# Clearing the warm-up tile first, and spare matmuls in TensorE's waits for the quarters of batch 0's x

## The chip, the core and the metric

The kernel runs on one core of a Trainium2 chip. The metric is the device time of one execution in microseconds; the time of before is the median of seven runs. The engines are named as in the profile: PE is TensorE's matmuls and PEld its weight loads, DVE is VectorE, ACT is ScalarE, POOL is GpSimd, SP is SyncE, which here only issues DMAs.

## The reference

Two stages. The first is an attention between x and a small state, in both directions; the second is a feed-forward layer with a snake activation over all resulting tokens.

```python
B, H, S, Ns, D = (8, 8, 512, 32, 64)
# attention: x is (B, H, S, D), state is (B, H, Ns, D)
scores = x @ state.T / sqrt(D);  a = softmax(scores);   xread = a @ state
scores2 = state @ x.T / sqrt(D); a2 = softmax(scores2); sread = a2 @ x
attn_out = concatenate([xread, sread], axis=2)          # (B, H, 544, 64)
x = attn_out.transpose(0, 2, 1, 3).reshape(4352, 512)
# feed-forward: d_model 512, d_ff 2048
h = x @ w_in
s = np.sin(alpha * h)
g = h + s * s / (alpha + 1e-09)
return (g @ w_out).astype(np.float32)                   # (4352, 512)
```

## The kernel before

The work is cut into steps, each a method of `Steps` that issues a few instructions. The list `ORDER` names them in one sequence with their arguments (`xq.3.A` is `xq(3, "A")`); each engine and each queue executes its own instructions in the order of this list, and waits on semaphores for what other engines make. Capital letters choose an engine (A ScalarE, V VectorE, G GpSimd, S the SP queue), and the last number of a step that writes PSUM is one of eight banks. Each bank holds one tile at a time: the next tile in it waits until the one before is done with.

Tokens are processed in nine groups: one for each batch (512 tokens) and one of all state reads (256 tokens). For a batch, x is transposed, the scores against the state are made (`sc`), their exponential (`ex`), its row sums (`rs`), reciprocals (`rr`) and the normalised weights (`nm`). These are transposed (`at` and `ac` for batch 0). Instead of reading the state and then multiplying with w_in, the kernel multiplies the state with w_in (`m`, evicted by `me`), and `h` or `hg` multiplies the weights with that product, 128 columns of d_ff at a time. `si` is the sine, `sq` its square, `gt` the snake sum, `o` the product with w_out, `oc` and `os` the eviction and the store.

The head, which the change edits, gets batch 0 ready. Its steps:

- `touch_x`, `touch`, `l_alpha`: three small DMAs that ScalarE issues. `l_s01`: the state of batches 0 and 1, on SP. `lq.0` to `lq.3`: four quarters of batch 0's x (two heads each), on SP.
- `consts` (line 209): DVE clears the tile `warm`, the operand of the warm-up matmuls, and fills `ones`. `zero.0` and `zero.1` (line 214): DVE clears `stT`, the transposed state, in two parts. `ident_` makes the identity on POOL, `identf` casts a corner of it on DVE.
- `warm_up.n.cols.bank` (line 303): n matmuls of `cols` columns over the cleared tile, into a bank that nobody reads.
- `exp_table`, `sin_table`: ScalarE loads the table for the exponential, later that for the sine.
- `s01_c`, `s01_t`, `s01_k`: the state of batches 0 and 1 is cast (POOL), transposed (TensorE, line 309) and copied into `stT` by DVE and ScalarE (line 316).
- `xq.q.A` (line 356): ScalarE casts a quarter of x when it has landed; `xtq.q` (line 361): TensorE transposes it, four matmuls; `xc` (line 385): the result is copied out of PSUM by DVE or ScalarE.
- `al_t`, `al_c`, `inva`: alpha is transposed (line 320), copied and inverted (DVE). `st_t`, `st_c`: the rest of the state is transposed (line 333) and copied into `stT` (line 340).
- `l_st`, `li`, `lo`, `lx`: DMAs of the state, w_in, w_out and the next batch's x, issued on POOL.

In before the list begins with `zero.1` ahead of `consts`; the warm-up is three pairs of 128 columns and six of 512; between the quarters of x there are no spare matmuls, but after quarter 3 there are ten, and more follow later.

```python
def warm_up(k, n, cols, bank):
    wp = k.ps(bank, [k.P, k.S], FP32, "warm_ps")
    for _ in range(n):
        k.nc.tensor.matmul(wp[:, :cols], k.warm[:, 0:k.P], k.warm[:, :cols], start=True, stop=True)
```

Of the kernel before, what the change touches and what calls it, by code (L numbers as in the profile page):

```python
# [18 lines left out]


ORDER = """
touch_x l_s01 zero.1 touch lq.0.S ident_ consts warm_up.2.128.0 warm_up.2.128.1 warm_up.2.128.2
l_alpha lq.1.S zero.0 warm_up.6.512.3 exp_table lq.2.S identf.V lq.3.S s01_c.G l_st li.0 xq.0.A
s01_t.4 li.1 xtq.0.5 xq.1.A s01_k.1.V s01_k.0.A li.2 xtq.1.6 xc.0.0.0.V xq.2.A xc.0.0.1.V lo.0
al_t.7 xq.3.A xtq.2.0 al_c inva sc.0.0.1 lo.1 xc.0.1.0.A xtq.3.2 warm_up.2.128.3 ex.0.0
warm_up.2.128.4 lx.1.0.1 warm_up.2.128.5 xc.0.1.1.V warm_up.2.128.6 warm_up.2.128.7 rs.0.0 sc.0.1.0
li.3 st_t.0.3 ex.0.1 rr.0.0 st_t.1.4 lo.2 st_c.0.0.V st_c.0.1.A warm_up.2.128.5 warm_up.2.128.6
warm_up.2.128.1 st_c.1.0.A rs.0.1 warm_up.2.128.2 warm_up.2.128.7 nm.0.0.0.4.G warm_up.2.128.0
warm_up.2.128.5 st_c.1.1.A warm_up.2.128.3 warm_up.2.128.6 warm_up.2.128.1 rr.0.1 warm_up.2.128.2
sin_table warm_up.2.128.7 warm_up.2.128.0 nm.0.1.0.4.G at.0.0.5 warm_up.2.128.3 ac.0.0.V m.0.0.6.4  # L30
m.1.0.1.2 lo.3 at.0.1.7 me.0.0.0.V me.0.0.1.A warm_up.2.128.0 warm_up.2.128.3 me.1.0.1.A ac.0.1.V
hg.0.2.0.5 me.1.0.0.V hg.0.1.0.4 hg.0.2.1 hg.0.1.1 hg.0.0.0.0 lx.2.0.1 si.0.2 hg.0.0.1 m.1.1.6.3
si.0.1 m.0.1.7.2 hg.0.3.0.1 me.0.1.1.A sq.0.2.V hg.0.3.1 sq.0.1.G me.1.1.0.V me.1.1.1.A
warm_up.2.128.2 gt.0.2 si.0.0 warm_up.2.128.2 warm_up.2.128.6 warm_up.2.128.3 warm_up.2.128.2
warm_up.2.128.6 me.0.1.0.A gt.0.1 sq.0.0.G m.0.2.3.2 si.0.3 m.1.2.5.6 hg.0.4.0.7 me.0.2.0.V
me.0.2.1.A hg.0.4.1 sq.0.3.G hg.0.6.0.4 me.1.2.1.V hg.0.6.1 si.0.4 hg.0.7.0.3 hg.0.11.0.2 me.1.2.0.V
si.0.6 hg.0.7.1 sq.0.4.G hg.0.5.0.6 gt.0.0 hg.0.5.1 si.0.7 hg.0.11.1 hg.0.8.0.5 hg.0.8.1 sq.0.6.A
gt.0.3 sq.0.7.G o.0.3.0.2.0 si.0.5 gt.0.4 o.0.3.2.3 o.0.0.0.2.1 si.0.11 o.0.0.2.3 gt.0.6 sq.0.5.G
o.0.0.3.4 o.0.2.0.1.7 si.0.8 o.0.3.3.5 sq.0.11.A gt.0.7 hg.0.9.0.4 sq.0.8.G o.0.2.1.2 gt.0.5
o.0.2.2.4 hg.0.9.1 gt.0.11 o.0.0.4.5 hg.0.10.0.3 si.0.9 o.0.2.4.5 gt.0.8 o.0.0.5.6 o.0.3.5.6  # L40
sq.0.9.A o.0.3.6.8 pk.1.0.V hg.0.10.1 xt.1.1.6 pk.1.1.V si.0.10 gt.0.9 xt.1.0.2 xc.1.1.0.A sq.0.10.G
o.0.2.5.6 xc.1.1.1.V xc.1.0.0.A o.0.0.6.7 xc.1.0.1.V o.0.0.7.8 o.0.2.6.7 sc.1.1.5 gt.0.10 sc.1.0.4
m.0.3.6.2 ex.1.0 o.0.2.7.8 me.0.3.0.V o.0.1.0.3.3 me.0.3.1.V o.0.1.3.6 hg.0.13.0.6 o.0.1.6.7 ex.1.1
# [620 lines left out]
```

## Time and profile before

| | us |
|---|---|
| median of 7 runs | 221.27 |
| lowest, highest | 221.04, 222.78 |
| the seven runs | 221.04, 221.16, 221.16, 221.27, 221.8, 222.75, 222.78 |
| the profiled execution | 221.38 |
| its span, from the first to the last instruction | 219.5 |

The profile is of one execution. Times in it are counted from its first instruction; a row of the timeline gives the start, the length, the engine, the line, the operation with output and inputs, and in brackets the idle time before it and what ended that. A row of the chain of work gives the start, the length, and the engine and line that held the end back in that stretch. Rows of a stage give busy time with the number of instructions, the granted TensorE clock, the DMA share and GB/s. Matmuls are pipelined, so the length of one is more than the distance to the next.

The page's groups have the warm-up in one row, 66 matmuls in all:

```profile
L303 PE MATMUL warm_ps<-warm 128*128 128x128 bf16 (+1 forms) x66 | 7.4, 265 | 2.2 <-DVE warm L209 2.0
```

### The profile page before, as it was taken

The page shows a single profiled execution, that of the slowest core. Times are in us where ns is not written, and L with a number is a line of the kernel's source. Part 1 is how long each engine was busy: PE and PEld are TensorE (multiplying, and loading weights), DVE is VectorE, ACT ScalarE, POOL GpSimd, SP SyncE. Part 2 cuts the span into 40 slices and gives each one's busy share as a digit, 9 for nine tenths or more (in the row PEclk, how much of TensorE's full clock was granted, in tenths as well). Part 3 has the DMA queues.
Part 4 walks back from the last instruction along what each step waited for, and adds up shares of the span by engine and source line. Part 5 has one row for each costly group of instructions (what it writes and reads, how often), then busy time and mean ns, then how long its engine had stood idle before and what let it go on. Part 6 is the DMA issues. An engine that isn't in the chain of part 4 may idle for free.

```text
span 219.5 us, 4330 instructions
## 1 busy us (share of the span) xinstructions
PE 213.1 (97%) x1619; PEld 104.8 (48%) x1619; DVE 162.4 (74%) x286; ACT 173.6 (79%) x297; POOL 107.2 (49%) x115
## 2 busy tenths in 40 slices
PE   6899999999999999999999999999999999999994
PEld 2744544444444534444454444444444555665452
DVE  2769896999668889989888788888667987671201
ACT  3799878997899979898996999798858896685111
POOL 5958534795296647743943387273501082121000
PEclk9999999999999999999999999999999999999999
DMA  5999999935378529167135327470220211012042
GB/s 176 202 207 203 205 203 122 215 127 96 99 157 131 99 79 151 53 151 90 53 73 126 114 76 96 130 114 0 48 100 0 99 48 48 0 51 96 1 143 96
DMA packets 38052, 23.48 MB, mean 107 GB/s; under 512 B 20992, under 2 KB 33680, under 8 KB 38032
## 3 DMA queue, kind: packets, MB, share of 16 engines
q0 software_dynamic: 11648, 8.13, 26.3%
q1 hardware_dynamic: 26128, 15.08, 26.1%
q8 instruction: 12, 0.20, 0.4%
q14 instruction: 8, 0.07, 0.1%
q10 hardware_dynamic: 256, 0.01, 0.1%
HBM read 17.44 MB, written 8.91 MB: 120 GB/s over the span
## 4 chain that ended last, share of the span: by engine, by line
PE 95%; ACT 3%; DVE 1%; issue 0%
PE o_ps L587 54%; PE h_ps L537 22%; PE m_ps L488 4%; PE h_ps L543 3%; PE h_ps L552 3%; PE warm_ps L303 3%; PE s_ps L399 2%; PE w_ps L450 2%; PE w_ps L461 1%; ACT L226 1%; ACT s L560 1%; ACT M L496 1%; PE x_ps L376 0%; PE st_ps L333 0%; ACT stT L340 0%; PE x_ps L361 0%
## 5 line engine op out<-in xcount | busy, mean ns | idle before, releaser
L587 PE MATMUL o_ps<-w_out_sb,gT 128*128 128x512 bf16 (+2 forms) x560 | 137.7, 373 | 0.0
L576 DVE SCALAR_TENSOR_TENSOR gT<-s,inva_sb,h_ps 128x512 bf16<-128x512 bf16 (+1 forms) x144 | 96.6, 714 | 18.9 <-POOL s L201 9.5
L201 POOL TENSOR_TENSOR s<-s 128x512 bf16<-128x512 bf16 (+1 forms) x76 | 76.7, 1021 | 63.8 <-ACT s L560 62.0
L560 ACT ACTIVATE s<-h_ps,alpha_sb 128x512 bf16<-128x512 f32 (+1 forms) x144 | 88.8, 671 | 10.5 <-PE h_ps L543 4.3
L587 PEld LDWEIGHTS <-gT 128*128 128x128 bf16 x560 | 52.3, 98 | 60.3 <-issue 5.0
L537 PE MATMUL h_ps<-AT,M 128*128 128x512 bf16 x224 | 60.8, 379 | 0.0
L537 PEld LDWEIGHTS <-M 128*128 128x128 bf16 x224 | 21.7, 98 | 25.9 <-issue 0.4
L569 ACT ACTIVATE s<-s 128x512 bf16<-128x512 bf16 (+1 forms) x53 | 31.4, 595 | 0.8
L201 POOL TENSOR_TENSOR A<-E,rR 128x512 bf16<-128x512 bf16 x16 | 16.6, 1049 | 23.9 <-ACT o_sb L595 12.7
L595 ACT COPY o_sb<-o_ps 128x512 f32<-128x512 f32 (+2 forms) x24 | 13.7, 572 | 16.6 <-PE o_ps L587 16.5
L496 ACT CAST M<-m_ps 128x512 bf16<-128x512 f32 x35 | 18.6, 593 | 8.2 <-PE m_ps L488 8.1
L496 DVE CAST M<-m_ps 128x512 bf16<-128x512 f32 x29 | 18.9, 680 | 2.4 <-PE m_ps L488 2.1
L595 DVE COPY o_sb<-o_ps 128x512 f32<-128x512 f32 x11 | 7.6, 691 | 13.0 <-PE o_ps L587 12.9
L410 DVE TENSOR_REDUCE R<-E 128x16 f32<-128x512 bf16 x16 | 10.4, 658 | 1.2 <-ACT E L406 0.9
L201 DVE TENSOR_TENSOR s<-s 128x512 bf16<-128x512 bf16 (+1 forms) x15 | 6.2, 415 | 6.8 <-ACT s L560 6.7
L488 PE MATMUL m_ps<-w_in_sb,stT 64*32 64x512 bf16 x256 | 10.2, 382 | 0.0
L468 DVE RECIPROCAL rC<-w_ps 128x128 f32<-128x128 f32 x8 | 7.6, 948 | 3.3 <-PE w_ps L461 3.2
L552 PE MATMUL h_ps<-AT,M 128*128 128x512 bf16 x32 | 9.4, 380 | 0.4 <-ACT M L496 0.4
L303 PE MATMUL warm_ps<-warm 128*128 128x128 bf16 (+1 forms) x66 | 7.4, 265 | 2.2 <-DVE warm L209 2.0
L406 ACT ACTIVATE E<-s_ps 128x512 bf16<-128x512 f32 x16 | 8.8, 602 | 0.4 <-PE s_ps L399 0.3
L543 PE MATMUL h_ps<-xs_all,w_in_sb 128*128 128x256 bf16 x64 | 9.1, 273 | 0.0
L560 ACT ACT_TABLE_LOAD x5 | 6.4, 1283 | 2.2 <-PE h_ps L537 1.1
(56 smaller groups left out, 101.8 us busy)
## 6 DMA issues: line engine op xcount, KB each, us to landing
out_dram<-o_sb SPq DMA_DIRECT2D x33, 256.0 KB, 2.3
xnat<-in_x_dram POOLq DMA_DIRECT2D x7, 512.0 KB, 7.6
w_in_sb<-in_moe_w_in_dram POOLq DMA_DIRECT2D x4, 512.0 KB, 10.8
w_out_sb<-in_moe_w_out_dram POOLq DMA_DIRECT2D x4, 512.0 KB, 17.4
x<-in_x_dram SPq DMA_DIRECT2D x4, 256.0 KB, 4.6
st_nat<-in_state_dram POOLq DMA_DIRECT2D x1, 256.0 KB, 5.2
out_dram<-o_sb SPq DMA_DIRECT2D x1, 192.0 KB, 1.9
s<-in_state_dram SPq DMA_DIRECT2D x1, 128.0 KB, 2.3
```

Source lines behind the costliest of these rows:

```text
L201: {"V": k.nc.vector, "G": k.nc.gpsimd}[eng].tensor_tensor(out, a, b, ALU.mult)
L303: k.nc.tensor.matmul(wp[:, :cols], k.warm[:, 0:k.P], k.warm[:, :cols], start=True, stop=True)
L488: k.nc.tensor.matmul(k.t["m", b, s + n, g][o0:o0 + k.Ns, :], k.stT[k.half(r), b * k.G + g, c0:c0 + k.Ns], k.w_in_sb[k.half(r), 2 * g + h, ...
L496: k.copy(eng)(k.t["M", b][:, g, s * k.FW:(s + 1) * k.FW], k.t["m", b, s, g][:])
L537: k.nc.tensor.matmul(hp[:, :n], k.t["M", t][:, g, fs], k.t["AT", t][:, g, :], start=(g == 0), stop=(g == k.G - 1),)
L543: k.nc.tensor.matmul(hp[:, :n], k.w_in_sb[:, q, fs], k.xs_all[:, q].rearrange("p b j -> p (b j)"), start=(q == 0), stop=(q == k.Q - 1),)
L552: k.nc.tensor.matmul(k.t["h", t, f][:], k.t["M", t][:, g, f * k.P:(f + 1) * k.P], k.t["AT", t][:, g, :], start=(g == 0), stop=(g == k.G - 1),)
L560: k.nc.scalar.activation(s[:, :n], k.t["h", t, f][:, :n], ACT.Sin, scale=k.alpha_sb[:, f:f + 1])
L569: k.nc.scalar.activation(s2[:, :n], s[:, :n], ACT.Square)
L576: k.nc.vector.scalar_tensor_tensor(gT[:, :n], k.t["s2", t, f][:, :n], k.inva_sb[:, f:f + 1], k.t["h", t, f][:, :n], ALU.mult, ALU.add,)
L587: k.nc.tensor.matmul(k.t["o", t, st, half][:, cols], k.t["gT", t, f][:, rows], k.w_out_sb[:, f, cols], start=(f == 0), stop=(f == k.FT - 1),)
L595: k.copy(eng)(o_sb[:, cols], k.t["o", t, st, half][:, cols])
```

## The change

Only the head of `ORDER` changes, up to `ex.0.0`; from there on the list is the same, though its lines are broken at other places. `consts` moves to the place of `zero.1`, and `zero.1` goes behind the warm-up. The six warm-up matmuls of 128 columns go, and six of 512 become seven. Fifteen matmuls of 128 columns in bank 3 are added: three after quarter 0's transposes, seven after quarter 1's, three after quarter 2's, and two before quarter 3's. No method changes.

```diff
-touch_x l_s01 zero.1 touch lq.0.S ident_ consts warm_up.2.128.0 warm_up.2.128.1 warm_up.2.128.2
-l_alpha lq.1.S zero.0 warm_up.6.512.3 exp_table lq.2.S identf.V lq.3.S s01_c.G l_st li.0 xq.0.A
-s01_t.4 li.1 xtq.0.5 xq.1.A s01_k.1.V s01_k.0.A li.2 xtq.1.6 xc.0.0.0.V xq.2.A xc.0.0.1.V lo.0
-al_t.7 xq.3.A xtq.2.0 al_c inva sc.0.0.1 lo.1 xc.0.1.0.A xtq.3.2 warm_up.2.128.3 ex.0.0
+touch_x l_s01 consts touch lq.0.S ident_ l_alpha lq.1.S zero.0 warm_up.7.512.3 exp_table lq.2.S
+zero.1 identf.V lq.3.S s01_c.G l_st li.0 xq.0.A s01_t.4 li.1 xtq.0.5 warm_up.3.128.3 xq.1.A
+s01_k.1.V s01_k.0.A li.2 xtq.1.6 warm_up.7.128.3 xc.0.0.0.V xq.2.A xc.0.0.1.V lo.0 al_t.7 xq.3.A
+xtq.2.0 warm_up.3.128.3 al_c inva sc.0.0.1 lo.1 xc.0.1.0.A warm_up.2.128.3 xtq.3.2 warm_up.2.128.3
+ex.0.0
...
```

More of the change, by code (lines that the diff above doesn't have):

```diff
@@ L21 @@
 ORDER = """
-touch_x l_s01 zero.1 touch lq.0.S ident_ consts warm_up.2.128.0 warm_up.2.128.1 warm_up.2.128.2
-l_alpha lq.1.S zero.0 warm_up.6.512.3 exp_table lq.2.S identf.V lq.3.S s01_c.G l_st li.0 xq.0.A
-s01_t.4 li.1 xtq.0.5 xq.1.A s01_k.1.V s01_k.0.A li.2 xtq.1.6 xc.0.0.0.V xq.2.A xc.0.0.1.V lo.0
-al_t.7 xq.3.A xtq.2.0 al_c inva sc.0.0.1 lo.1 xc.0.1.0.A xtq.3.2 warm_up.2.128.3 ex.0.0
-warm_up.2.128.4 lx.1.0.1 warm_up.2.128.5 xc.0.1.1.V warm_up.2.128.6 warm_up.2.128.7 rs.0.0 sc.0.1.0
-li.3 st_t.0.3 ex.0.1 rr.0.0 st_t.1.4 lo.2 st_c.0.0.V st_c.0.1.A warm_up.2.128.5 warm_up.2.128.6
@@ L28 @@
[L28 to L39, printed above, removed]
@@ L40 @@
-o.0.2.2.4 hg.0.9.1 gt.0.11 o.0.0.4.5 hg.0.10.0.3 si.0.9 o.0.2.4.5 gt.0.8 o.0.0.5.6 o.0.3.5.6
+touch_x l_s01 consts touch lq.0.S ident_ l_alpha lq.1.S zero.0 warm_up.7.512.3 exp_table lq.2.S
+zero.1 identf.V lq.3.S s01_c.G l_st li.0 xq.0.A s01_t.4 li.1 xtq.0.5 warm_up.3.128.3 xq.1.A
+s01_k.1.V s01_k.0.A li.2 xtq.1.6 warm_up.7.128.3 xc.0.0.0.V xq.2.A xc.0.0.1.V lo.0 al_t.7 xq.3.A
+xtq.2.0 warm_up.3.128.3 al_c inva sc.0.0.1 lo.1 xc.0.1.0.A warm_up.2.128.3 xtq.3.2 warm_up.2.128.3
+ex.0.0 warm_up.2.128.4 lx.1.0.1 warm_up.2.128.5 xc.0.1.1.V warm_up.2.128.6 warm_up.2.128.7 rs.0.0
@@ new lines @@
+sc.0.1.0 li.3 st_t.0.3 ex.0.1 rr.0.0 st_t.1.4 lo.2 st_c.0.0.V st_c.0.1.A warm_up.2.128.5
+warm_up.2.128.6 warm_up.2.128.1 st_c.1.0.A rs.0.1 warm_up.2.128.2 warm_up.2.128.7 nm.0.0.0.4.G
+warm_up.2.128.0 warm_up.2.128.5 st_c.1.1.A warm_up.2.128.3 warm_up.2.128.6 warm_up.2.128.1 rr.0.1
+warm_up.2.128.2 sin_table warm_up.2.128.7 warm_up.2.128.0 nm.0.1.0.4.G at.0.0.5 warm_up.2.128.3
+ac.0.0.V m.0.0.6.4 m.1.0.1.2 lo.3 at.0.1.7 me.0.0.0.V me.0.0.1.A warm_up.2.128.0 warm_up.2.128.3
+me.1.0.1.A ac.0.1.V hg.0.2.0.5 me.1.0.0.V hg.0.1.0.4 hg.0.2.1 hg.0.1.1 hg.0.0.0.0 lx.2.0.1 si.0.2
@@ new lines @@
+hg.0.0.1 m.1.1.6.3 si.0.1 m.0.1.7.2 hg.0.3.0.1 me.0.1.1.A sq.0.2.V hg.0.3.1 sq.0.1.G me.1.1.0.V
+me.1.1.1.A warm_up.2.128.2 gt.0.2 si.0.0 warm_up.2.128.2 warm_up.2.128.6 warm_up.2.128.3
+warm_up.2.128.2 warm_up.2.128.6 me.0.1.0.A gt.0.1 sq.0.0.G m.0.2.3.2 si.0.3 m.1.2.5.6 hg.0.4.0.7
+me.0.2.0.V me.0.2.1.A hg.0.4.1 sq.0.3.G hg.0.6.0.4 me.1.2.1.V hg.0.6.1 si.0.4 hg.0.7.0.3 hg.0.11.0.2
+me.1.2.0.V si.0.6 hg.0.7.1 sq.0.4.G hg.0.5.0.6 gt.0.0 hg.0.5.1 si.0.7 hg.0.11.1 hg.0.8.0.5 hg.0.8.1
+sq.0.6.A gt.0.3 sq.0.7.G o.0.3.0.2.0 si.0.5 gt.0.4 o.0.3.2.3 o.0.0.0.2.1 si.0.11 o.0.0.2.3 gt.0.6
@@ L41 @@
+sq.0.5.G o.0.0.3.4 o.0.2.0.1.7 si.0.8 o.0.3.3.5 sq.0.11.A gt.0.7 hg.0.9.0.4 sq.0.8.G o.0.2.1.2
+gt.0.5 o.0.2.2.4 hg.0.9.1 gt.0.11 o.0.0.4.5 hg.0.10.0.3 si.0.9 o.0.2.4.5 gt.0.8 o.0.0.5.6 o.0.3.5.6
 sq.0.9.A o.0.3.6.8 pk.1.0.V hg.0.10.1 xt.1.1.6 pk.1.1.V si.0.10 gt.0.9 xt.1.0.2 xc.1.1.0.A sq.0.10.G
```

## The prediction

> **What bounds the kernel now.** I read the page's busy shares first, then the chain of work that ended last, then the timeline of the first 20 us, because the diff touches nothing later than `ex.0.0`.
>
> ```profile
> span 219.5 us, 4330 instructions
> PE 213.1 (97%) x1619; PEld 104.8 (48%) x1619; DVE 162.4 (74%) x286; ACT 173.6 (79%) x297; POOL 107.2 (49%) x115
> PE 95%; ACT 3%; DVE 1%; issue 0%
> ```
>
> TensorE is the bound, and it has no idle time after 17 us: its waits, by the view of waits, are 2.0 (start), 0.6, 0.4 and 0.2 us. So whatever the head gains or loses at 17 us moves the end by as much, and what is hidden before that moves nothing. What paces the head is in the chain of its first 18 us:
>
> ```profile
> 0.97 0.70 DVE stT L214
> 1.67 0.28 DVE warm L209
> 2.00 3.38 PE warm_ps L303 x12
> 5.38 0.59 PE st_ps L309 x8
> ...
> 6.82 0.61 ACT xp L356
> 7.43 0.05 issue
> 7.47 0.40 PE x_ps L361 x4
> 7.87 0.25 PE s_ps L399 x8
> 8.12 0.04 issue
> 8.15 0.40 PE x_ps L361 x4
> 8.55 0.56 PE warm_ps L303 x10
> ...
> 16.69 0.29 PE warm_ps L303 x2
> 16.98 0.04 issue
> 17.02 0.72 PE warm_ps L303 x10
> ```
>
> The chain passes through the memset of `stT` (0.70), the warm-up (3.38) and the state transposes, and this looks like 0.7 us to be had. It is not, because ScalarE's casts of x wait for something else, as the timeline of ScalarE and TensorE shows:
>
> ```profile
> 4.24 0.62 ACT L356 CAST xp<-x 128x512 bf16<-128x512 f32 x1 [0.58 <-DMA x<-in_x_dram]
> 5.57 0.62 ACT L356 CAST xp<-x 128x512 bf16<-128x512 f32 x1 [0.72 <-DMA x<-in_x_dram]
> 6.80 1.30 ACT L356 CAST xp<-x 128x512 bf16<-128x512 f32 x2
> 7.47 0.40 PE L361 MATMUL x_ps<-ident,xp 128*128 128x128 bf16 x4 [0.65 <-ACT xp L356]
> ```
>
> The quarters of x are cast as they land, at about 4.2, 5.55, 6.78 and 7.46 us. The casts end 4.86, 6.19, 7.42 and 8.10, and TensorE can transpose a quarter some 0.05 later. Quarters 2 and 3 are transposed at 7.47 and 8.15, at once after their casts: from 6.78 us on, the DMA paces the head, not the warm-up.
>
> The last thing to read is TensorE's own rate. The granted clock reads 1.000 in all the profile, and the page's row shows 9 throughout, yet the early matmuls run at half rate. The weight loads ahead of the 512-column warm-ups start 0.43 us apart (the timeline), while ten later 512-column matmuls take 2.16 us in the chain, 0.216 each. Four transposes of a quarter, by stages of line 361 (PE busy, count):
>
> ```profile
> 3.04 0.15 PEld L303 LDWEIGHTS <-warm 128*128 128x128 bf16 x1 [0.27 <-issue]
> 3.47 0.15 PEld L303 LDWEIGHTS <-warm 128*128 128x128 bf16 x1 [0.28 <-issue]
> 3.89 0.15 PEld L303 LDWEIGHTS <-warm 128*128 128x128 bf16 x1 [0.28 <-issue]
> ```
> ```profile
> 5.87:6.27 0.40, 0.39 (x4) 1.00 0.95 230
> 7.46:7.69 0.23, 0.22 (x4) 1.00 0.98 160
> ```
>
> 0.107 us each before 6.27, 0.056 after. The full rate came at about 6.27 us, 4.3 us after the first matmul.
>
> **The change part by part.**
>
> *Clearing the tile first.* `consts` goes ahead of `zero.1`. DVE does the same five small jobs, 0.97 to 2.31, in both orders; the warm tile is ready at 1.24 instead of 1.94, and the first matmul starts at 1.30 instead of 2.00. What is now late is `stT` (ready near 2.3 instead of 1.67); its first other writer is DVE at 5.99, so that costs nothing. Steps that `zero.1` is moved past issue on other engines (loads of x on SP, of alpha and w_in on ScalarE, the exp table, the identity on POOL); no queue's own order changes, and no DMA is added. The exp table's read of the tile comes at 3.46, after the tile is ready in both.
>
> *The warm-up.* Six of 128 columns (6 x 0.107 = 0.64) are replaced by one more of 512 (0.43): 7 x 0.427 = 2.99, so it ends at 4.29 instead of 5.20. The state transposes then run 4.40 to 4.83 (before 5.31 to 5.73; their cast was done at 3.45), those of quarter 0 at 4.91 to 5.34 (its cast ends 4.86; before 5.88). This 0.97 us is lost again at quarter 1, whose cast ends at 6.19: its transposes start at 6.24, before at 6.28. Gain on the path: nothing, covered by the landings. Were that cover gone, it would be up to 0.97.
>
> *The spare matmuls*, 15 of 128 columns. Three after quarter 0: 5.34 to 5.66 at half rate, into a wait that lasts until 6.24; free, but 0.58 us stays empty. Seven after quarter 1 (done 6.47 at full rate): 0.39, to 6.86; free. Behind them waits alpha's transpose (before 6.60, now near 6.9), and behind that DVE's copy of it at 7.15, which was held there by other work: 0 to 0.1 later, with 0.45 idle before DVE's next urgent job at 8.59. Three after quarter 2 (7.47 to 7.70): to 7.86; the scores of group 0 behind them are done at 8.10 instead of 7.93, and their exponential waits for ScalarE until 8.48 anyway. Two before quarter 3: to 8.21. Here the cover ends: quarter 3 could start at 8.15. So +0.06. From there to the state's transposes TensorE has no wait (8.15 to 10.37), and their first copy by DVE at 10.00 has some 0.02 to spare: +0.04 to +0.06 at the end.
>
> *Bank 3.* All the spares write bank 3. What a group costs that must wait for the one before it in its bank shows at 16.69: two matmuls, the next group at 17.02, so a bank comes free about 0.27 after the start of its last matmul. The pair before quarter 3 needs it at 8.10 (free 8.08), the pair after it at 8.43 (free 8.42): 0 to 0.1, I take 0.
>
> *The rate.* This is what the trace can't show. Bounds: full rate as early as now or earlier, nothing (the landings stand); a gain is excluded, since everything TensorE does before 7.47 already ends ahead of its landing. Later, the price is that of half rate on the chain after 6.27. [...]
>
> Which of them? The trace: full rate 4.3 us after the first matmul. Carried over plainly that gives 5.6 us, and no cost. [...] By the trace's rule the sum is +0.05[...]. The runs of before speak for two kinds: five at 221.04 to 221.8, two at 222.75 and 222.78. I take the release in time in most runs, as before[...].
>
> *Sum.* +0.05 on the profiled execution's 221.38 (span 219.5) is 221.43. That execution stands 0.11 above the median of 221.27, so 221.3 as a median. This likeliest case by itself: 220.9 to 221.8, the width of before's lower five runs.
>
> **The rivals.**
>
> *Slower: the release misses.* [...] It gives 222.5 to 222.9. It decides the median once more than half of the runs miss. For: [...] before's two slow runs of 222.8. Against: TensorE starts 0.7 us sooner, and after 6.24 it is full.
>
> *Faster: the head moves as a whole.* If the quarters land sooner than in this execution, the warm-up is what paces the head, and 0.97 us for quarter 0 and the 0.2 of its transposes at full rate come through: 221.38 - 1.17, or 220.1 to 220.2. Against: both waits of ScalarE for x (0.58, 0.72) and that no DMA is moved.
>
> *Nothing reached.* The three spares end 0.58 short of quarter 1, so that wait is filled by a third only; then the change is the likeliest case with +0.05, same time.
>
> **How the numbers follow.** About 0.5% (1.1 us) is what a measurement of this kernel can tell from no change: below 220.16 faster, above 222.38 slower. The likeliest case with the third rival, all within it: 0.60. The release missed in most runs: 0.28. The head moved whole: 0.12. Leaving out the last, and the top of the second, the range is 220.7 to 222.9.
>
> **What would show it.** Right: first warm-up matmul at 1.3, quarter 0's transposes near 4.9, quarter 1's at 6.2 with about 0.6 idle before them, quarters 2 and 3 at 7.5 and 8.2, x landing as before, the state's transposes at 9.3 to 9.4, four transposes of quarter 2 in 0.22. Wrong to the slow side: quarter 2's four take 0.4 and the state's transposes start after 10.3. Wrong to the fast side: the state's transposes before 9, with quarter 3 landed before 7. A shift that arises after 17 us would fall outside all of this.

## The result and the profile after

The changed kernel takes 224.11 us (median of 12 runs, 223.45 to 226.0), where before took 221.27 (31 runs by then). The ratio is 1.0117 with a 95% interval of 1.0093 to 1.0141: slower, above the range of the prediction (220.7 to 222.9). The profiled execution took 224.07 with a span of 221.0, so 1.5 us of its loss lie inside the span and the other 1.2 outside it. A second profile of the same kernel (224.64) has a span of 222.5, and there nearly all of the loss is inside.

Outside the span the trace of after has three packets of program code, 2.2 to 2.3 us after the last instruction; that of before has none. The queues of after from 221.1 to 225 us:

```profile
q14 instruction: 2, 0.02, 1.7%
q8 instruction: 1, 0.02, 1.6%
```

The time less the span is 1.8 to 1.9 us in every run of before whose span is on record, and 2.5 to 3.3 us in three of after's twelve. That these late fetches cost the 1.2 us was not tested.

The page of after, its first part and the engines of the chain that ended last:

```profile
span 221.0 us, 4350 instructions
PE 214.3 (97%) x1629; PEld 105.6 (48%) x1629; DVE 162.6 (74%) x286; ACT 173.4 (78%) x297; POOL 107.1 (48%) x115
PE 90%; DMA 5%; ACT 3%; SPq 1%; issue 0%
```

Two DMAs have come into the chain. One is the landing of quarter 2's x, which the chain of the head now passes through where it passed through the warm-up before. No time is lost by it; it is the landing that the prediction named as the head's pace.

```profile
2.17 4.43 DMA x<-in_x_dram
```

The head's timeline has the steps that were forecast, most of them a little early:

```profile
1.19 3.17 PE L303 MATMUL warm_ps<-warm 128*128 128x512 bf16 x7 [1.19 <-DVE warm L209]
5.11 0.61 PE L361 MATMUL x_ps<-ident,xp 128*128 128x128 bf16 x4 [0.19 <-ACT xp L356]
5.83 0.63 PE L361 MATMUL x_ps<-ident,xp 128*128 128x128 bf16 x4
7.30 0.40 PE L361 MATMUL x_ps<-ident,xp 128*128 128x128 bf16 x4
8.04 0.39 PE L361 MATMUL x_ps<-ident,xp 128*128 128x128 bf16 x4
9.17 1.08 PE L333 MATMUL st_ps<-ident,st_nat 128*64 128x128 bf16 x32
```

Quarter 1 is transposed at 5.83 instead of 6.24, because its x had landed by 5.0 and not at 5.55, so the 0.58 of idle time that was forecast before it is not there. The state's transposes start at 9.17, 0.12 before those of before. TensorE then runs 0.11 ahead of before, instruction for instruction, until 75 us; from the scores of batch 4 on it is 1.57 behind. The view of TensorE's waits (us in total, times, longest) tells what comes there:

```profile
PE s_ps L399 <- DMA xT<-xp: 1.5, 1, 1.5
PE warm_ps L303 <- DVE warm L209: 1.2, 1, 1.2
PE h_ps L552 <- ACT M L496: 0.4, 1, 0.4
```

In the chain of work this is the second DMA, one piece between the last matmul that didn't need it and the scores of batch 4:

```profile
70.79 0.04 PE o_ps L587
70.83 5.96 DMA xT<-xp
76.79 0.05 issue
76.84 0.64 PE s_ps L399 x16
```

This is `td.4`, the DMA on SP that transposes batch 4's x, which neither the diff nor the prediction mentions. From issue to landing it takes, by the view of the tile `xT` from 70 to 77 us, first before, then after:

```profile
DMA to landing us min/median/max: 4.3/4.3/4.3
```
```profile
DMA to landing us min/median/max: 6.0/6.0/6.0
```

To the hundredth, 4.25 and 5.96. Its data packets are not slower: in before the last one starts 3.77 us after the issue, in after 3.92. What is late are its last two completion writes, of 4 bytes each. The view of the DMA queues, after, 74.6 to 75.6 us, and then 75.6 to 75.8:

```profile
GB/s 31 11 0 10 10 20 666 0 0 0 0 0 0 0 0 0 0 0 0 0 0 0 0 0 0 0 0 0 0 0 0 0 0 0 0 0 0 0 0 0
q8 instruction: 1, 0.02, 5.9%
q1 hardware_dynamic: 13, 0.00, 1.5%
```
```profile
DMA packets 2, 0.00 MB, mean 0 GB/s; under 512 B 2, under 2 KB 2, under 8 KB 2
q1 hardware_dynamic: 2, 0.00, 1.4%
```

The one packet of `q8 instruction` is a fetch of program code: 16,384 bytes, starting at 74.77 (the slice of 666 GB/s), the moment the last data packets are through, and taking 0.94. The two completion writes start at 75.69 and 75.70, just before it ends. In before the code fetch that corresponds starts at 76.42, 1.2 us after this DMA has landed:

```profile
GB/s 0 0 0 0 546 0 0 0 0 0 0 0 0 0 0 0 0 0 0 0 0 0 0 0 0 0 0 0 0 0 0 0 0 0 0 0 0 0 0 0
q8 instruction: 1, 0.02, 5.3%
```

(the queues of before from 76.3 to 77.5). Why would a change in the first 9 us move a fetch at 76? The change adds ten matmuls on balance, each with its weight load: twenty instructions of TensorE. Everything behind them sits twenty places further on in TensorE's program. The theory was that the fetch is tied to a place in that program, which TensorE now reaches twenty places sooner; the rivals were that the head shifts the DMAs in time, and that the length of the program counts as such.

### The profile page after: what moved, and what is told of

Its sections match the earlier page's. It is cut to its first block, busy times and chain, and to the rows that moved or that the text cites. A ratio compares the mean times of both kernels' runs of the same rounds, so it can differ in the third digit from the quotient of the medians.

```text
span 221.0 us, 4350 instructions
## 1 busy us (share of the span) xinstructions
PE 214.3 (97%) x1629; PEld 105.6 (48%) x1629; DVE 162.6 (74%) x286; ACT 173.4 (78%) x297; POOL 107.1 (48%) x115
## 4 chain that ended last, share of the span: by engine, by line
PE 90%; DMA 5%; ACT 3%; SPq 1%; issue 0%
PE o_ps L587 52%; PE h_ps L537 21%; PE m_ps L488 4%; PE h_ps L543 3%; DMA xT<-xp 3%; PE h_ps L552 3%; DMA x<-in_x_dram 2%; PE s_ps L399 2%; PE w_ps L450 2%; PE w_ps L461 1%; PE warm_ps L303 1%; ACT L226 1%; ACT s L560 1%; ACT M L496 1%; PE x_ps L376 0%; PE st_ps L333 0%
## 5 line engine op out<-in xcount | busy, mean ns | idle before, releaser
L303 PE MATMUL warm_ps<-warm 128*128 128x128 bf16 (+1 forms) x76 | 9.0, 264 | 1.4 <-DVE warm L209 1.2
```

## The experiments

Two tools need a word. A pair of spare matmuls of 128 columns can be merged into one of 256, or cut into four of 64: the same columns, but one matmul fewer, or two more (two or four instructions, with the weight loads). So the program's length changes and the columns that TensorE works through do not, and only spares behind `st_c.0.0` were used for it; for the longest cut in length (e8) also those behind `ex.0.0`.

**Same head, same length as before (e1).** Ten pairs merged:

```diff
-... st_c.0.0.V st_c.0.1.A warm_up.2.128.5 warm_up.2.128.6 warm_up.2.128.1 ...
+... st_c.0.0.V st_c.0.1.A warm_up.1.256.5 warm_up.1.256.6 warm_up.1.256.1 ...
```

> After's head as it is; behind it, ten of the spare pairs of two matmuls of 128 columns become one matmul of 256 columns, so TensorE's work stays and its program has as many instructions as before's. Code-position theory (a fetch of TensorE's code lands on the end of the fourth batch's transposing DMA): the fetch goes back to some 1.6 us behind that DMA's end, the wait of 1.5 us in the scores of batch 4 is gone, about 221.2 to 221.4. Theory that the head itself (its start 0.1 us earlier, other overlap of DMAs) makes that DMA late: the wait stays, about 224.

221.19 us, ratio to before 0.9988 (0.9968 to 1.0008). With after's whole head the loss is gone; the DMA takes 4.25 again and TensorE's view of waits has no line for it.

**Before's head, longer program (e2).** The converse, five pairs cut:

```diff
-... st_c.0.0.V st_c.0.1.A warm_up.2.128.5 warm_up.2.128.6 warm_up.2.128.1 ...
+... st_c.0.0.V st_c.0.1.A warm_up.4.64.5 warm_up.4.64.6 warm_up.4.64.1 ...
```

> Before with five of its later spare pairs of 128 columns cut into four matmuls of 64, so ten matmuls (twenty instructions, with their weight loads) more and the same columns; the head is before's. Code-position theory: as slow as after, about 224, with a wait of some 1.5 us for the transposing DMA of batch 4. Head theory: as before, about 221.3.

224.13 us (five runs), ratio 1.0114 (1.006 to 1.0167): after's loss without after's head. Its waits show both places:

```profile
PE s_ps L399 <- DMA xT<-xp: 1.3, 1, 1.3
PE h_ps L537 <- DMA AT<-A: 1.1, 1, 1.1
```

The second is `ad.1`, the transposing DMA of batch 1's weights. It lands 5.14 after its issue, where before has 3.15. A code fetch starts at 35.08, between its issue (34.72) and its first data (35.99), where before has it at 39.70, after that DMA has landed. But this fetch is over at 36.20, before the data are through (37.45), so it does not stand between data and completion as at batch 4, and what delays this DMA is not shown.

The profile is of the slowest of the five runs (226.05), and 1 us of its loss has another cause. TensorE comes late to its full rate, in before's own head: the four transposes of quarter 2 take 0.40 instead of 0.22, and the state's transposes start at 10.28 instead of 9.29.

```profile
7.38:7.79 0.41, 0.40 (x4) 1.00 1.10 190
10.28 0.64 PE L333 MATMUL st_ps<-ident,st_nat 128*64 128x128 bf16 x8
```

**Clearing first, nothing else (e3).**

```diff
-touch_x l_s01 zero.1 touch lq.0.S ident_ consts warm_up.2.128.0 ...
+touch_x l_s01 consts touch lq.0.S ident_ warm_up.2.128.0 ...
-l_alpha lq.1.S zero.0 warm_up.6.512.3 exp_table lq.2.S identf.V ...
+l_alpha lq.1.S zero.0 warm_up.6.512.3 exp_table lq.2.S zero.1 identf.V ...
```

> Only the warm-up tile is cleared first; no matmul is added or taken away. Code-position theory: as before, 221.1 to 221.4, since TensorE's program is the same. Theory that an earlier start shifts the DMAs into each other: 224, or at least over 222.4.

Ratio 1.0004 (0.9978 to 1.003): no effect clear of the noise. Its median, 221.69, lies above what was expected, but the interval holds 1. Of an earlier start by itself no effect can be told, in either direction.

**After again (e4).** For a second profile.

> After, unchanged, for a second profile: its median stands 2.8 us above before's, its profiled execution only 1.6 with the wait of batch 4. Code-position theory: the same wait at batch 4 again, and where this execution's span is nearer 222, a second wait for a transposing DMA with a code fetch on it. Head theory: the rest lies in the head.

224.62 us (five runs), ratio 1.0123 (1.0077 to 1.0169). Both waits are there, and the span is 222.5:

```profile
PE s_ps L399 <- DMA xT<-xp: 1.7, 1, 1.7
PE h_ps L537 <- DMA AT<-A: 0.9, 1, 0.9
```

So the loss inside the span has up to two parts: 1.3 to 1.7 at batch 4, which every profile at this length shows where the scores stand in their place, and about 1 at batch 1, which this one and that of e2 show and the first one does not.

**Cover for the wait (e6).** The scores of batch 4 go behind other work of TensorE; the program stays as long as after's.

```diff
-... o.2.0.11.12 sc.4.0.5 sc.4.1.6 gt.2.14 o.2.3.10.12 ex.4.0 o.2.3.12.13 w.1.2 cs.1 o.2.0.12.13 rc.1 ...
+... o.2.0.11.12 gt.2.14 o.2.3.10.12 o.2.3.12.13 w.1.2 cs.1 o.2.0.12.13 sc.4.0.5 sc.4.1.6 ex.4.0 rc.1 ...
```

> After, with the scores of batch 4 moved behind some 1.7 us of TensorE's other work (o.2.3, w.1, cs.1, o.2.0); its program is as long as after's. Code-position theory: the DMA still lands late, but TensorE has work until then: 1.2 to 1.5 us less than after, 222.4 to 223. Theory that the loss is not in this wait: as after, 224.1 or more.

222.35 us, ratio 1.0043 (1.0022 to 1.0064), 1.8 us less than after and a little more than expected. The DMA is still late (5.94), but TensorE no longer waits for it (the scores' weight loads start at 77.84, just after the landing at 77.80). Of the two waits for a DMA the profile keeps only the one at batch 1:

```profile
PE h_ps L537 <- DMA AT<-A: 1.1, 1, 1.1
```

So by runs some 1.8 of after's 2.8 us are the wait at batch 4. The rest lies at batch 1 and outside the span (4 of the 13 runs have 2.4 to 3.8 us there), and these two were not split.

**How far must the fetch move? (e5)** Two pairs merged, four instructions fewer than after.

> After with two of its later spare pairs merged into one matmul of 256 columns each, so only four instructions of TensorE fewer than after. Code-position theory: at batch 4 two matmuls of 0.22 us move the fetch some 0.4 us back, behind the last completion writes of the transposing DMA, so the wait of 1.5 us there goes; the wait of 0.9 to 1.1 us at batch 1 (its transposing DMA lands near 37, the fetch starts near 33.6) may stay. About 222, between 221.3 and 222.6. If instead the length of the program counted as such, or the head, four of twenty instructions would take a fifth of the loss: about 223.6.

A miss: 224.5 us (five runs), ratio 1.0144 (1.0114 to 1.0174), the whole loss. The fetch starts at 74.45, 3.92 after the DMA's issue, as in after (3.94), and not 0.4 later. In both it starts within 0.02 us of the last data packet. What ties it to that packet is not shown, and it is not always so: in before, the fetch at 143.31 starts in the midst of the data of the transposing DMA issued at 140.55. The author's guess from this was a step theory: what counts is only whether the fetch is asked for while the DMA runs. There are 1206 instructions of TensorE (matmuls and weight loads) ahead of the scores of batch 4 in this kernel, 1210 in after, 1190 in before.

**The step, from three sides (e9, e10, e11).** Six pairs merged (1198 instructions ahead of the scores); four pairs cut (1226); ten pairs cut (1250).

> After with six later spare pairs merged: twelve instructions of TensorE fewer, 1198 ahead of the scores of batch 4 (before 1190, after 1210, the kernel with four fewer 1206). Step theory (the fetch is asked for when TensorE's instruction stream passes a fixed place; if that place lies ahead of the scores of batch 4, it is asked for while the transposing DMA runs and gets between its data and its last completion writes; if it lies behind, only after the DMA has landed): either the whole 1.5 us at batch 4 or none of it, so about 224 or, with what batch 1 costs, 221.3 to 222.6. Slope theory (the loss goes with the number of instructions): about 222.8, with a wait of some 0.6 us at batch 4.

> After with four later spare pairs cut into four matmuls of 64 columns each: sixteen instructions of TensorE more, the same columns. Step theory: the fetch is asked for some 1.7 us earlier than in after; if that is still inside the transposing DMA, the loss stays whole, about 224; if it is ahead of the DMA's data, the wait at batch 4 goes. Slope theory: more than after, about 226.

> After with ten later spare pairs cut into four matmuls of 64 columns: forty instructions of TensorE more, the same columns. Step theory: the fetch is asked for some 4 us earlier than in after, ahead of the transposing DMA's data at batch 4, so the wait there goes although the program is longer: 221.3 to 222.6. Slope theory: over 227.

All three fell as a step and not as a slope. With 1198 the loss is gone: 221.31, ratio 0.9972 (0.9954 to 0.9989). With 1226 the DMA takes 5.92, TensorE waits 1.5, and the time is 223.17, ratio 1.0074 (1.0046 to 1.0103). That is less than after; its profile has no wait at batch 1, and none of its runs loses time outside the span. With 1250, the longest program of all, the wait at batch 4 is gone again, since the fetch now comes ahead of the DMA (issued at 71.34); its queues from 70.8 to 71.9 us:

```profile
GB/s 0 0 596 0 0 0 0 0 0 0 0 0 0 0 0 0 0 0 0 0 0 0 0 0 0 0 0 0 0 0 0 0 0 0 0 0 0 0 0 0
q8 instruction: 1, 0.02, 5.7%
```

Its ratio is 1.001 (0.9989 to 1.0031), though its profile has 0.7 us of waiting at batch 1.

The same profile has batch 4's picture a second time, at another DMA: a transposing DMA issued at 118.62 meets a code fetch 2.70 us later, within 0.02 us of its last data packet. Its last two completion writes start just before the fetch ends, and it lands after 4.77 us, where the thirteen other profiles, without a fetch there, have 3.04 to 3.06. Nothing on TensorE waits for it.

**A shorter program (e8)**, twenty pairs merged:

> After with twenty spare pairs merged, forty instructions of TensorE fewer than after and twenty fewer than before. Code-position theory: at batch 4 the fetch comes later still than in before, clear of the DMA, and at batch 1 too: 221.0 to 221.4. Theory that fewer instructions are simply less work: below before by about what after is above it, near 219.

221.34 us, ratio 0.9999 (0.9985 to 1.0013). Twenty instructions fewer than before buy nothing by their number.

**A version to beat both.** First e1 with the scores of batch 4 moved as in e6 (e7), then e9 once more (e12):

> After's head, ten spare pairs merged (before's number of instructions), and the scores of batch 4 behind 1.7 us of other work: the version meant to beat both. Code-position theory: 220.9 to 221.2, and few or none of its runs over 222.5, where before has 7 of 33, if those come from the same DMA. Otherwise as before, with the same share over 222.5.

> The kernel with twelve instructions fewer than after, unchanged, once more: it was 0.28% below before (0.11 to 0.46). If the earlier warm-up and the spares gain something when the fetch is out of the way: 0.1 to 0.5% below before again, 220.6 to 221.1 where before is 221.2. If the first comparison was chance: 221.2, an interval that holds 1.

e7 gives 1.0007 (0.9989 to 1.0024), no gain, and 4 of its 21 runs lie above 222.2: before's runs near 222.7 have a cause that covering this DMA doesn't remove. e12 gives 221.16, ratio 0.9979 (0.9962 to 0.9995), after 0.9972 in e9. So after with six pairs merged is some 0.2% faster than before, close to what can be told at all. The difference lies in a group of before's runs near 222.7: 19 of its 46 runs beside e9 and 9 of its 27 beside e12 are above 222.3, and no run of e9 or e12 is above 222.1. Without that group the medians of before are 221.2, those of e9 and e12 221.3 and 221.2. Why the group is missing was not isolated.

All kernels together, ordered by the number of TensorE's instructions ahead of the scores of batch 4 (in e7 and e6 these scores were moved, so they are counted to where they stood; where a trace lacks records of matmuls, the count is that of the edit); times from the records of the trace, relative to the issue of `td.4`:

| kernel | instructions | code fetch starts | td.4 lands | ratio to before |
|---|---|---|---|---|
| e8 | 1170 | 5.40 | 4.27 | 0.9999 |
| before | 1190 | 5.45 | 4.25 | 1 |
| e3 | 1190 | 5.22 | 4.25 | 1.0004 |
| e1 | 1190 | 5.40 | 4.25 | 0.9988 |
| e7 | 1190 | 4.50 | 4.25 | 1.0007 |
| e9 | 1198 | 5.24 | 4.28 | 0.9972 |
| e12 (e9 again) | 1198 | 5.40 | 4.27 | 0.9979 |
| e5 | 1206 | 3.92 | 5.94 | 1.0144 |
| after | 1210 | 3.94 | 5.96 | 1.0117 |
| e4 (after again) | 1210 | 3.94 | 5.94 | 1.0123 |
| e2 | 1210 | 3.86 | 5.92 | 1.0114 |
| e6 | 1210 | 3.92 | 5.94 | 1.0043 |
| e10 | 1226 | 3.92 | 5.92 | 1.0074 |
| e11 | 1250 | -0.48 | 4.25 | 1.001 |

At this DMA there are two landing times and nothing between them. Elsewhere there is a third case: where a fetch starts 0.01 us behind the last completion writes, the landing is 0.2 late (e11's transposing DMA at 50.89: 4.47).

## Why the prediction was wrong

**What held.** Clearing first moved the first matmul to 1.19 (1.30 forecast) and gained nothing (e3). Quarter 2 is transposed at 7.30 (7.47 forecast), as soon as its cast allows. Quarter 3 follows at 8.04 (8.21 forecast), 0.17 after its cast ended at 7.87: here the spares ahead of it do cost something, as forecast. The forecast of +0.05 for the head was of the right size and the wrong sign in this execution (-0.12). That is in part chance, since x landed earlier than in before (quarter 2 at 6.60 and not 6.78), which the prediction took as fixed. For e1, which has the whole head, the ratio is 0.9988, with an interval that holds 1. The full rate came at about 6.6 us, when the starts of the spares go from 0.107 to 0.056 apart (one takes 0.31 before that and 0.22 after). Two stages of line 361, quarter 0 and quarter 2 (PE busy, count), show half and full rate.

```profile
5.10:5.50 0.40, 0.39 (x4) 1.00 0.92 323
7.29:7.52 0.23, 0.22 (x4) 1.00 1.11 174
```

That is 5.4 us after the first matmul, where before had 4.3; in e6 quarter 0, from 4.64, already runs at full rate. So a fixed 4.3 us from the first matmul, which the prediction carried over from before, does not hold. What brings the full rate on is not shown by any of these profiles, and the slower rival's 222.5 to 222.9 rests on an estimate of the author's that no trace showed. The cost stayed nothing all the same, because the landings covered it (quarter 2's x landed at 6.60).

The slower rival (a missed release of the rate) is refuted as the cause of after's loss, although its sign was right: its mark, quarter 2 in 0.4 and the state's transposes after 10.3, is absent. Only e2's profile comes near it, with before's head. The faster rival did not happen in this execution: quarter 3 still landed after 7. Its mark does show in five later profiles with after's head (e1, e7, e8, e11, e12): quarter 3 lands between 6.5 and 6.9 there, and the state's transposes start between 8.65 and 8.96. So the head gains up to 0.6 where x lands early; by the times of these kernels it can't be told.

**The step that failed** is the sum of the spares: each was priced by its time on TensorE (0.107 or 0.056 us), and hidden time was taken as free. A matmul also takes two places in the program (the page of after has 1629 matmuls and 1629 weight loads). The sum should have had one more line, "+10 matmuls, +20 instructions, code fetches come sooner". That line was put at nothing, and by itself it measured 1.5 us in the profile and 1.8 by runs (e6), with up to 1 us more at batch 1 and at times 1.2 outside the span. With it fell "whatever the head gains or loses at 17 us moves the end by as much": after was 0.11 ahead at 17 us and 1.5 behind at the end. The sentence "no queue's own order changes, and no DMA is added" overlooked a queue that the page of before lists: `q8 instruction`, twelve packets and 0.20 MB. The view of TensorE's waits, which the prediction read, lists no wait of a matmul for this DMA. But the timeline of before has the weight loads of batch 4's scores waiting for it:

```profile
75.26 0.52 PEld L399 LDWEIGHTS <-xT 128*128 128x128 bf16 x16 [0.32 <-DMA xT<-xp]
```

The scores start at 75.27, 0.05 after the landing, so this DMA had no slack at all. The prediction ended with "a shift that arises after 17 us would fall outside all of this"; all of it did.

The twelve packets of before are of 16,384 bytes each. From the first (12.97) to the last (193.85) TensorE starts 2686 matmuls and weight loads, so by estimate a fetch comes with every 244 of them; in after, where twelve start inside the span, it is 2660 and 242. TensorE's own waits name no code in these profiles, and the line of waits that after has and before has not is for the transposing DMA, which lands 1.7 us late (5.96 and 4.25 after its issue). At batch 4 a single packet of 0.94 us stands between its data and its last two completion writes. Why the fetch started only at the end of the data there is not shown, nor is which DMA engine served which packet.

**What stays open.** The fetch takes 0.94, but the DMA lands 1.7 later than in before, and its landing follows the last completion write by 1.1 instead of 0.47; where the other 0.6 comes from is not shown. Nor is the exact place that asks for the fetch: by an estimate from e9 and e5 it would be one of the 1199th to the 1206th of TensorE's instructions, if the stream stands still at the scores until their DMA has landed, which fits fetches 1.0 to 1.2 after the landing in before, e1, e3, e8 and e9, but was not tested by itself. Batch 1 waits in some profiles of the same kernel and not in others. Its transposing DMA lands 4.7 to 5.2 after the issue in e2, e4, e6 and e11, where the code fetch starts 0.28 to 0.57 after the issue, and 3.2 to 3.6 in after, e5 and e10, where it starts at 0.24 to 0.27; in all seven the fetch is over before the data are. The 1.2 us outside the span are open too. More than 2.3 us outside it are found only in runs of after, e4, e2, e5, e6 and e9, whose programs for TensorE have 3246 to 3258 matmuls and weight loads, and in no run of a shorter (before: 3238) or longer one (e10: 3274, e11: 3298). The group of before's runs near 222.7 was not profiled; executions in which the full rate comes late could be part of it (in e2's profile the state's transposes start at 10.28, 0.99 later than in before), but this was not tested.

## What to carry to other kernels

A filler instruction that costs no time still costs a place in the program. Here twenty of them moved a code fetch from 76.42 to 74.77 us, and TensorE then waited 1.5 for a DMA: after adding or removing instructions in a program like this one, look at where its code fetches fall against DMAs that end just in time. Before forecasting no change, list the waits with no slack, however far behind the edit they lie; this DMA was needed 0.05 us after it landed. If a harmless edit loses a microsecond far from itself, restore the instruction count with the edit kept (merge or cut some spares) before blaming the edit; e1, which did so, took 0.9988 of before's time where after took 1.0117.

## What was not expected of the hardware

One code fetch of 16 KiB (16,384 bytes), 0.94 us long, makes a transposing DMA land 1.7 us late (5.94 after issue, and not 4.25), and at this DMA it does so in whole or not at all: eight instructions, 1198 or 1206 ahead of the scores, decide over some 1.5 us of waiting, and forty more than after has take the wait away again.
